# The even sums of block 12 made on GpSimd: one line of an order written out by hand

## The chip, the cores and the metric

The kernel runs on one core of a Trainium2 chip. A core has five engines that run their own instruction streams and wait for one another through semaphores: TensorE (PE in the profile, its weight loads PEld), VectorE (DVE), ScalarE (ACT), GpSimd (POOL) and SyncE (SP, which here issues nearly all of the transfers). The metric is the device time of one execution in microseconds (us). The time before the change is 439.48 us, the median of three runs (439.42 to 439.49).

## The reference

The reference is a spectral mixing layer followed by a gated feed-forward layer, in float32, on one sequence of 2048 rows of 512 numbers:

```python
def _A_ref(x, w_r, w_i):
    X = rfft2(x); W = w_r + 1j * w_i
    return irfft2(X * W, (S, D))
def _B_ref(x, w_gate, w_up, w_down):
    h = gelu(x @ w_gate) * (x @ w_up)
    return h @ w_down
h  = x + _A_ref(layernorm(x), A_w_r, A_w_i)
h2 = h + _B_ref(layernorm(h), B_w_gate, B_w_up, B_w_down)
```

So the first half normalizes every row, takes a two-dimensional Fourier transform over rows and columns, multiplies by a filter, transforms back and adds the input. The second half normalizes again, multiplies by two matrices (512 x 1376), gates, and multiplies back.

## The kernel before

The 2048 rows lie as 16 blocks of 128 rows, one row of each block per partition. The Fourier transforms are products with small tables of cosines and sines on TensorE. The kernel goes through these stages: a transform over the rows, block by block (called the first stage here); a transform over the columns, the filter and the inner transform back (the second stage, lines 427 to 474); the transform back over the rows (lines 535 and 874); and the feed-forward layer, which takes most of the time (lines 165 to 167, 774 and 1113).

In the first stage a block b goes through these steps, each of which has a letter in a list called START; a letter followed by a number is one step on one block:

- `f`: the fold. A row's 512 numbers are cut into two halves, and their difference and their sum are written to the tile `pn` (lines 340 and 341). Blocks 12 and 13 are folded together by one pair of instructions, and so are 2 and 3, 4 and 5, and so on up to 10 and 11; blocks 0, 1, 14 and 15 are folded alone. GpSimd does it for all but block 15, which VectorE folds (ON_VECTOR).
- `v`: the second fold. VectorE takes the difference of the two quarters of `pn` and writes it to `uv` (line 351), for both blocks of a pair at once. The odd column frequencies need it.
- `u`: the second sum. The two quarters of `pn` of one block are added and written to `us` (line 361). The even column frequencies can be made from it. It is an optional step: only blocks 13, 14 and 15 have it before the change, on VectorE.
- `s`, `g`, `m`, `q`, `r`, `n`: the mean and the variance of the rows and the root of the variance; `c`: the table of cosines and sines of the block is multiplied by that root and written to `ms` (line 332, on ScalarE).
- `a`: the even frequencies on TensorE (line 374), and `b`: the odd ones. `b` is two products of 128 by 128. `a` is two products where the block has had its step `u`, and four where it has not, because then the two quarters are added up by TensorE in PSUM, each quarter with a product of its own. TensorE takes a float32 product as two records in the profile, so two products are a row `x4` there and four are `x8`.
- `k`: ScalarE copies the block's bank of PSUM to the tile `ts` (line 382); for block 15 half of it is copied by VectorE (`l`, line 385), after a small memset of a PSUM region (`z`, line 389).

What makes the sum `u` is in these lines:

```python
us = w1.tile([P, 2, P], F32, name="us", bufs=5)
eng = pool if b in SUMS_ON_POOL else dve
eng.tensor_tensor(us, pn[:, :, 0], pn[:, :, 1], op=ALU.add)
parts[b][:2] = [[us[:, 0]], [us[:, 1]]]
```

The order of the steps on TensorE, ScalarE, VectorE and GpSimd is the order of START, word for word: each engine takes its own steps in the order in which they stand there, and waits at a step until what the step reads is there. On GpSimd there are also two small additions for the filter's edge columns (`wh`, line 483), which belong to the second stage and stand in the program right behind the fold of block 14; behind them come the subtractions that prepare the weights of the feed-forward layer (`raw`, lines 209 to 217), and the first of these waits for the last second fold on VectorE (line 351).

The second stage begins with line 427 on TensorE, which reads `ts` of all blocks. Its first products need the copies of the even half of block 15, which VectorE makes (line 385), and ScalarE's copies of all earlier blocks.

Of the kernel before, what the change touches and what calls it, by code (L numbers as in the profile page):

```python
# [35 lines left out]
START = """  # L36
f0 s0 g0 r0 n0 s1 c0 v0 g1 s2 m3 q3 r1 g2 f1 v1 n1 r2 m5 c1 q5 n2 c2 m7 c3 f2 s4 s6 g4 a0 b0 w7 g6 v2 q7 r4 n4 m9 c4
s8 c5 c6 q9 a1 a2 b1 a3 f4 f6 m11 b2 k0 v4 s10 q11 g10 g8 c7 v6 b3 a4 f8 a5 b5 b4 r8 k2 k1 n8 c8 s12 f10 a6 m13 c9 c10
c11 k4 a7 b7 f12 f14 q13 s15 v8 g12 s14 k3 b6 k7 g15 a8 a9 k5 g14 r12 v10 n12 b8 v12 b9 k9 c12 a11 u13 c13 a10 b10 u14
k8 f15 b11 a12 b12 k6 a13 k10 c14 c15 k11 v14 u15 b13 k13 k12 v15 a14 b14 a15 b15 z4 l15 k14 k15  # L40
"""

ON_POOL = ()

ON_VECTOR = (15,)

SUMS_ON_POOL = ()

ROOTS = {0: 1, 1: 1, 2: 2, 4: 4, 8: 4, 12: 4}

# [71 lines left out]
def kernel(  # L122
# [114 lines left out]
    with (  # L237
# [119 lines left out]
        def sums2(b):  # L357
            pn = pns[group[b][0]][:, b - group[b][0]]
# [3 lines that stand above are left out]
# [1074 lines left out]
```

## Time and profile before

| what | value |
|---|---|
| median of three runs | 439.48 us |
| the profiled execution | 439.26 us |
| its span, first to last instruction | 437.0 us |
| TensorE busy | 431.5 us, 99% of the span |
| GpSimd busy, VectorE busy, ScalarE busy | 314.4, 312.6 and 242.8 us |
| first product of the first stage (line 374) | at 7.50 us |
| first product of the second stage (line 427) | at 29.97 us |

Times in the profile count from the first instruction of the span. A row of the timeline gives the start, the duration, the engine, the line, the operation, what it writes and reads, the shape, and, in brackets at the end, how long the engine had been idle before it and what ended that. Instructions of one kind that follow each other are merged into one row (`x4`). Instructions overlap a little at their ends, so the step from one start to the next tells the pace of an engine better than a duration does, above all for TensorE. The chain of work that ended last is followed back from the last instruction, at each step to whatever released it.

### The profile page before, as it was taken

The page shows a single profiled execution, that of the slowest core. Times are in us where ns is not written, and L with a number is a line of the kernel's source. Part 1 is how long each engine was busy: PE and PEld are TensorE (multiplying, and loading weights), DVE is VectorE, ACT ScalarE, POOL GpSimd, SP SyncE. Part 2 cuts the span into 40 slices and gives each one's busy share as a digit, 9 for nine tenths or more (in the row PEclk, how much of TensorE's full clock was granted, in tenths as well). Part 3 has the DMA queues.
Part 4 walks back from the last instruction along what each step waited for, and adds up shares of the span by engine and source line. Part 5 has one row for each costly group of instructions (what it writes and reads, how often), then busy time and mean ns, then how long its engine had stood idle before and what let it go on. Part 6 is the DMA issues. An engine that isn't in the chain of part 4 may idle for free.

```text
span 437.0 us, 6628 instructions
## 1 busy us (share of the span) xinstructions
PE 431.5 (99%) x2275; PEld 367.4 (84%) x2275; DVE 312.6 (72%) x578; ACT 242.8 (56%) x503; POOL 314.4 (72%) x346
## 2 busy tenths in 40 slices
PE   8999999999999999999999999999999999999996
PEld 8999999789978777877888888888888888888885
DVE  5979976898764766378735579478677787687786
ACT  5989685799802441124432786376455653575640
POOL 6988896999957788558653844067879779787821
PEclk9999999999999999999999999999999999999999
DMA  8996914220032122112230203401212021200005
GB/s 285 392 413 77 398 35 152 109 73 24 1 121 97 49 71 75 48 49 72 72 73 24 73 25 127 162 16 57 73 48 73 29 69 49 72 25 2 0 2 193
DMA packets 23542, 41.60 MB, mean 95 GB/s; under 512 B 4178, under 2 KB 9810, under 8 KB 23380
## 3 DMA queue, kind: packets, MB, share of 16 engines
q1 hardware_dynamic: 23220, 40.92, 27.8%
q8 instruction: 18, 0.29, 0.3%
q10 hardware_dynamic: 288, 0.26, 0.2%
q14 instruction: 16, 0.13, 0.1%
HBM read 36.97 MB, written 4.20 MB: 94 GB/s over the span
## 4 chain that ended last, share of the span: by engine, by line
PE 98%; issue 0%; DVE 0%; ACT 0%; POOL 0%; DVEq 0%; POOLq 0%
PE ps L165 16%; PE ps L166 16%; PE ps L167 16%; PE ps L774 14%; PE ps L1113 11%; PE ps L374 5%; PE ps L427 3%; PE ps L535 3%; PE ps L442 3%; PE ps L469 3%; PE ps L176 2%; PE ps L874 2%; PE ps L982 1%; PE ps L1219 1%; PE ps L568 1%; PE ps L574 1%
## 5 line engine op out<-in xcount | busy, mean ns | idle before, releaser
L165 PE MATMUL ps<-cb,gu 128*128 128x512 f32 (+1 forms) x336 | 127.4, 379 | 0.0
L167 PE MATMUL ps<-cb,gu 128*128 128x512 f32 (+1 forms) x336 | 124.9, 372 | 0.0
L166 PE MATMUL ps<-cb,gu 128*128 128x512 f32 (+1 forms) x336 | 124.8, 371 | 0.0
L678 ACT ACTIVATE s<-ps 128x512 f32<-128x512 f32 (+1 forms) x72 | 40.2, 560 | 87.2 <-PE ps L167 86.9
L230 POOL TENSOR_TENSOR gu<-raw,gu 128x768 fp32r<-128x768 f32 (+1 forms) x42 | 61.3, 1479 | 30.3 <-DVE gu L225 17.7
L165 PEld LDWEIGHTS ps<-cb,gu 128*128 128x128 f32 x336 | 63.3, 188 | 11.8 <-issue 1.0
L166 PEld LDWEIGHTS ps<-cb,gu 128*128 128x128 f32 x336 | 63.3, 188 | 11.7 <-issue 1.0
L167 PEld LDWEIGHTS ps<-cb,gu 128*128 128x128 f32 x336 | 63.2, 188 | 11.0
L774 PE MATMUL ps<-wd,a 128*128 128x512 f32 x264 | 63.6, 393 | 0.0
L774 PEld LDWEIGHTS ps<-wd,a 128*128 128x128 f32 x264 | 49.2, 188 | 11.5 <-DVE gh L983 0.9
L687 DVE TENSOR_TENSOR ps<-ps,s 128x512 f32<-128x512 f32 (+1 forms) x48 | 31.2, 651 | 27.8 <-PE ps L167 25.7
L1120 DVE TENSOR_TENSOR gh<-ps,gh 128x512 f32<-128x512 f32 x66 | 44.2, 680 | 0.8 <-PE ps L1113 0.8
L684 ACT ACTIVATE s<-s 128x512 f32<-128x512 f32 (+1 forms) x48 | 28.5, 594 | 20.6 <-DVE s L681 20.5
L780 DVE TENSOR_TENSOR gh<-ps,gh 128x512 f32<-128x512 f32 x24 | 16.5, 689 | 27.0 <-PE ps L774 26.9
L681 DVE TENSOR_TENSOR s<-ps,s 128x512 f32<-128x512 f32 (+1 forms) x48 | 30.8, 641 | 5.9 <-PE ps L167 4.7
L516 POOL TENSOR_TENSOR wd<-wdr,wd 128x512 fp32r<-128x512 f32 x12 | 15.5, 1294 | 18.9 <-ACT wd L514 18.9
L681 DVE TENSOR_TENSOR ps<-ps,s 128x512 f32<-128x512 f32 (+1 forms) x24 | 15.7, 652 | 16.8 <-ACT s L678 16.6
L1026 POOL TENSOR_TENSOR t<-mis,t 128x768 fp32r<-128x768 f32 (+1 forms) x9 | 13.3, 1480 | 13.3 <-ACT t L1024 13.2
L693 ACT ACTIVATE a<-ps 128x512 fp32r<-128x512 f32 (+1 forms) x26 | 13.7, 532 | 15.6 <-DVE ps L687 15.6
L458 POOL TENSOR_TENSOR z<-t,t 128x520 f32<-128x520 f32 x15 | 19.5, 1297 | 2.7 <-DVE t L450 2.1
L209 POOL TENSOR_TENSOR raw<-raw 128x256 f32<-128x256 f32 x16 | 11.8, 739 | 12.4 <-DMA raw<-in_wgu 10.7
L434 ACT ACTIVATE dp<-ps 64x512 f32<-64x512 f32 x30 | 17.7, 591 | 4.8 <-PE ps L427 4.5
(184 smaller groups left out, 899.3 us busy)
## 6 DMA issues: line engine op xcount, KB each, us to landing
wt<-in_w SPq DMA_DIRECT2D x16, 520.0 KB, 7.4
raw<-in_wgu SPq DMA_DIRECT2D x32, 256.0 KB, 3.0
out<-gh SPq DMA_DIRECT2D x15, 256.0 KB, 2.0
gh<-in_x SPq DMA_DIRECT2D x7, 512.0 KB, 9.1
row<-in_x SPq DMA_DIRECT2D x12, 256.0 KB, 2.7
wdr<-in_wd SPq DMA_DIRECT2D x12, 256.0 KB, 2.7
mis<-in_wd SPq DMA_DIRECT2D x10, 256.0 KB, 2.5
a<-in_wgu SPq DMA_DIRECT2D x8, 256.0 KB, 3.1
```

The costliest lines, as they stand in the source:

```text
L165: pe.matmul(o, lh, rh, start=(i == 0 and not onto), stop=False, skip_group_check=True)
L166: pe.matmul(o, lh, rl, start=False, stop=False, skip_group_check=True)
L167: last = pe.matmul(o, ll, rh, start=False, stop=(i == n - 1), skip_group_check=True)
L230: pooled["lo"] = pool.tensor_tensor(r[:, 1, m], t[:, m], r[:, 0, m].bitcast(F32), op=ALU.subtract)
L374: pe.matmul(spectrum(b, c)[:, c], o, mc, start=(z == 0), stop=(z == len(parts[b][c]) - 1))
L678: return lambda: act.activation(to, a, AF.Copy)
L681: return lambda: dve.tensor_tensor(to, a, b, op=ALU.add)
L684: return lambda: act.activation(g, g, AF.Gelu_apprx_tanh)
L687: return lambda: dve.tensor_tensor(u, u, g, op=ALU.mult)
L774: pe.matmul(o, parts_of[tiles.index((0, f))][:, ha, i // 4, r], wds[f][:, hw, c], start=start, stop=stop)
L1113: pe.matmul(ps[:, k], w[:, hw], a[ha], start=start and hw + ha == 0, stop=hw == 1, skip_group_check=True)
L1120: by.tensor_tensor(to, o, to, op=ALU.add)
```

## The change

Block 12 gets a step `u`, on GpSimd, and its step `a` moves to a later place among TensorE's steps. In the list START the step `u12` is put in behind `a11`, and `a12` is moved from between `b11` and `b12` to behind `b13`.

```diff
-c11 k4 a7 b7 f12 f14 q13 s15 v8 g12 s14 k3 b6 k7 g15 a8 a9 k5 g14 r12 v10 n12 b8 v12 b9 k9 c12 a11 u13 c13 a10 b10 u14
-k8 f15 b11 a12 b12 k6 a13 k10 c14 c15 k11 v14 u15 b13 k13 k12 v15 a14 b14 a15 b15 z4 l15 k14 k15
+c11 k4 a7 b7 f12 f14 q13 s15 v8 g12 s14 k3 b6 k7 g15 a8 a9 k5 g14 r12 v10 n12 b8 v12 b9 k9 c12 a11 u12 u13 c13 a10 b10
+u14 k8 f15 b11 b12 k6 a13 k10 c14 c15 k11 v14 u15 b13 a12 k13 k12 v15 a14 b14 a15 b15 z4 l15 k14 k15
...
-SUMS_ON_POOL = ()
+SUMS_ON_POOL = (12,)
```

On TensorE, at the end of the first stage, the rows are the products of blocks 11, 10, 12, 13, 14 and 15, in the order of the program; a row names the table (`ms`), the folded data (`pn`, `uv` or `us`) and the number of products. `pn_340` and `uv_379` belong to blocks 12 and 13, `ms_384` is the table of block 12. Before:

```order
L374 MATMUL ps_72<-ms_329,uv_372 128x128 x2
L374 MATMUL ps_72<-ms_331,uv_372 128x128 x2
L374 MATMUL ps_72<-ms_384,pn_340 128x128 x4
L374 MATMUL ps_72<-ms_384,uv_379 128x128 x2
L374 MATMUL ps_72<-ms_392,us_390 128x128 x2
L374 MATMUL ps_72<-ms_392,uv_379 128x128 x2
L374 MATMUL ps_72<-ms_418,us_400 128x128 x2
L374 MATMUL ps_72<-ms_418,uv_423 128x128 x2
L374 MATMUL ps_72<-ms_420,us_425 128x128 x2
```

These rows are b10, b11, a12, b12, a13, b13, a14, b14 and a15. The same place in the changed kernel, where the sums of blocks 12, 13, 14 and 15 are `us_390`, `us_392`, `us_402` and `us_423`:

```order
L374 MATMUL ps_72<-ms_329,uv_372 128x128 x2
L374 MATMUL ps_72<-ms_331,uv_372 128x128 x2
L374 MATMUL ps_72<-ms_384,uv_379 128x128 x2
L374 MATMUL ps_72<-ms_394,us_392 128x128 x2
L374 MATMUL ps_72<-ms_394,uv_379 128x128 x2
L374 MATMUL ps_72<-ms_384,us_390 128x128 x2
L374 MATMUL ps_72<-ms_416,us_402 128x128 x2
L374 MATMUL ps_72<-ms_416,uv_421 128x128 x2
L374 MATMUL ps_72<-ms_418,us_423 128x128 x2
```

The four products of a12 are gone from their place ahead of b12, and two products that read `us_390` stand between b13 and a14.

On GpSimd, at the end of its folds, this is the difference between the two programs, with one row more in the changed one:

```order
 L341 TENSOR_TENSOR pn_343<-gh_58 128x256
 L483 TENSOR_TENSOR wh_447<-ws_133 128x16x4 x2
+L361 TENSOR_TENSOR us_390<-pn_340 128x256
 L209 TENSOR_TENSOR raw_135<-raw_135 128x256
 L213 TENSOR_TENSOR raw_135<-raw_135 128x256
```

The new sum stands behind the fold of block 14 and behind the two additions for `wh`, and ahead of the preparation of the weights. VectorE, ScalarE and SyncE have the same rows in the same order in both programs.

## The prediction

> **What bounds the kernel now.** I read the page's busy times first, then the chain of work that ended last, then the timeline of TensorE, VectorE and GpSimd where the first stage ends. The page:
>
> ```profile
> span 437.0 us, 6628 instructions
> PE 431.5 (99%) x2275; PEld 367.4 (84%) x2275; DVE 312.6 (72%) x578; ACT 242.8 (56%) x503; POOL 314.4 (72%) x346
> PE 98%; issue 0%; DVE 0%; ACT 0%; POOL 0%; DVEq 0%; POOLq 0%
> ```
>
> TensorE is busy 99% of the span and holds 98% of the chain. So a delay of TensorE early on is carried to the end, unless a later stretch of the chain waits for something that isn't delayed. These are the longest pieces of the chain that are not TensorE's work after 25 us:
>
> ```profile
> 72.54 0.88 ACT gh L474 x2
> 123.67 0.76 DVE gh L983
> 432.58 0.57 issue
> 433.15 0.41 DVE gh L1224
> 433.57 0.33 DVEq L1428
> ```
>
> None of them is a transfer; each works on what TensorE has just made. Next, TensorE's rows where the change is made:
>
> ```profile
> 25.14 1.06 PE L374 MATMUL ps<-ms,pn 128*128 128x128 f32 x8
> 26.04 0.61 PE L374 MATMUL ps<-ms,uv 128*128 128x128 f32 x4
> 26.75 0.68 PE L374 MATMUL ps<-ms,us 128*128 128x128 f32 x4
> 27.27 0.61 PE L374 MATMUL ps<-ms,uv 128*128 128x128 f32 x4
> 27.71 0.61 PE L374 MATMUL ps<-ms,us 128*128 128x128 f32 x4
> 28.25 0.71 PE L374 MATMUL ps<-ms,uv 128*128 128x128 f32 x4
> 28.80 0.61 PE L374 MATMUL ps<-ms,us 128*128 128x128 f32 x4
> 29.24 0.61 PE L374 MATMUL ps<-ms,uv 128*128 128x128 f32 x4
> 29.97 0.35 PE L427 MATMUL ps<-dfs,ts 128*128 128x128 f32 x1
> ```
>
> In order these are a12, b12, a13, b13, a14, b14, a15, b15 and the second stage's first product. The starts give the pace: 8 records (a12) take 0.90 us, 4 records 0.44 (27.27 to 27.71). There are three waits: b12's four slots were over at 26.48 and a13 began at 26.75; a14 was done at 28.15 and b14 began at 28.25; L427 began 0.29 after b15's last slot (29.68). What was waited for stands on the other engines (the GpSimd row at 28.94 is the first preparation of the weights):
>
> ```profile
> 24.45 0.73 POOL L340 TENSOR_TENSOR pn<-gh 128x256 f32<-128x256 f32 x1
> 24.52 1.20 DVE L351 TENSOR_TENSOR uv<-pn 128x512 f32<-128x512 f32 x1 [0.68 <-POOL pn L341]
> 25.14 1.18 POOL L341 TENSOR_TENSOR pn<-gh 128x256 f32<-128x256 f32 x1
> 25.65 0.95 DVE L361 TENSOR_TENSOR us<-pn 128x256 f32<-128x256 f32 x1
> 26.28 0.50 POOL L483 TENSOR_TENSOR wh<-ws 128x64 f32<-128x64 f32 x1
> 26.52 0.53 DVE L361 TENSOR_TENSOR us<-pn 128x256 f32<-128x256 f32 x1
> 26.74 0.50 POOL L483 TENSOR_TENSOR wh<-ws 128x64 f32<-128x64 f32 x1
> 26.98 0.54 DVE L340 TENSOR_TENSOR pn<-gh 128x256 f32<-128x256 f32 x1
> 27.44 0.41 DVE L341 TENSOR_TENSOR pn<-gh 128x256 f32<-128x256 f32 x1
> 27.78 0.41 DVE L351 TENSOR_TENSOR uv<-pn 128x256 f32<-128x256 f32 x1
> 28.11 0.41 DVE L361 TENSOR_TENSOR us<-pn 128x256 f32<-128x256 f32 x1
> 28.45 0.41 DVE L351 TENSOR_TENSOR uv<-pn 128x256 f32<-128x256 f32 x1
> 28.94 0.72 POOL L209 TENSOR_TENSOR raw<-raw 128x256 f32<-128x256 f32 x1 [1.70 <-DVE uv L351]
> 29.07 0.07 DVE L389 MEMSET ps<- 128x16 f32 x1 [0.21 <-ACT ts L382]
> 29.44 0.42 DVE L385 COPY ts<-ps 128x256 f32<-128x256 f32 x1 [0.30 <-PE ps L374]
> ```
>
> VectorE's rows are v12 (24.52, for blocks 12 and 13), u13, u14, the two folds of block 15, v14, u15, v15, the memset and the copy l15. GpSimd's are the fold of block 14, the two `wh`, and the weights. a13 waited for u13, which ended at 26.60; b14 for v14 (28.19); L427 for l15 (29.86).
>
> The same rows show how the two engines get in each other's way. Alone, a sum of 128x256 takes VectorE 0.41 us (27.44) and GpSimd 0.73 (24.45). Side by side they take turns: the second half of f14 on GpSimd spans 1.18 us and ends 0.60 after v12 (26.32 against 25.72); u13 then spans 0.95 and ends 0.28 after it (26.60); `wh`, u14, `wh` and the first fold of block 15 go on in the same way, the last two ending at 27.24 and 27.52. So an instruction of one engine holds the other's up until it is nearly over.
>
> **The change part by part.**
>
> *Products taken out.* a12 falls from 8 records to 4: 0.90 - 0.45 = 0.45 us less work. Where it stood, nothing is gained by that. b12 now follows b11 at 25.14 and needs v12, which still ends at 25.72; with 0.06 to 0.15 of handing over (v14 ended at 28.19 and b14 began at 28.25; u13 ended at 26.60 and a13 began at 26.75) it begins near 25.85 and is done near 26.38. a13 still waits for u13 and begins at 26.75 as before, since nothing ahead of u13 on VectorE or GpSimd changes. So the old four products of a12 ran in time in which TensorE has to wait for VectorE in any case, and the new two come behind that wait.
>
> *The floor of the loss.* Suppose u12 were ready when TensorE gets there, at 27.71 behind b13. Then a12, a14 and b14 take 3 x 0.45 and a15 begins at 29.05 instead of 28.80. The wait and the slow restart at b14 (28.15 to 28.25, and 0.55 instead of 0.45 for its records, 0.20 in all) are covered by the 0.45 of a12, so 0.25 is left as a loss.
>
> *When u12 is ready.* On GpSimd it stands behind the second `wh`. That ends at 27.24, and by then the first fold of block 15 has been waiting on VectorE since 26.98. By the taking of turns in the rows above VectorE goes next, until 27.52, and u12 ends 0.60 later as f14 did behind v12: 28.12. The trace has no sum of two quarters on GpSimd. Its lower bound is the 0.73 of a fold of the same size alone (27.24 + 0.73 = 27.97, if it gets in ahead of VectorE), the upper one 27.52 + 0.73 = 28.25, if it can't begin before VectorE's fold is over. I take 28.12, since the nearest row, a GpSimd sum of the same size right behind a VectorE sum, has just this case.
>
> *The wait that is added.* a12 begins at 28.12 + 0.06 = 28.18, so TensorE waits 0.47 behind b13. Behind a12 on TensorE stand a14, b14, a15, b15 and the whole second stage. With a restart like that of b14 (0.55 from 28.25 to 28.80) a14 begins at 28.73, b14 at 29.17, a15 at 29.62. Before, a15 began at 28.80: 0.82 later. l15 and L427 follow a15 at the same distance, so L427 begins at 30.79.
>
> *What u12 does to VectorE.* The second fold of block 15 asks at 27.44, is held until u12 is over and ends 0.28 after it, at 28.40 instead of 27.85. v14, u15 and v15 move by the same 0.55 and end at 28.74, 29.08 and 29.41. They are wanted at 29.17 (b14), 29.62 (a15) and 30.06 (b15), so they cost nothing, with 0.4 to 0.6 us to spare. The weights on GpSimd wait for v15 and begin 0.55 later too, while TensorE and all that it releases move by 0.82, so this is covered by a quarter of a microsecond more than before.
>
> *Copies and the memset.* ScalarE's copies of k13, k12 and k14:
>
> ```profile
> 27.91 1.68 ACT L382 ACTIVATE ts<-ps 128x512 f32<-128x512 f32 x3 [0.82 <-PE ps L374]
> ```
>
> Their order stays. k12 now waits for a12, whose records are done at 28.18 + 0.71 = 28.89, and ends after its 0.56 (a third of the row) near 29.5; the memset follows it at 29.6, ahead of l15, which can't begin before a15's records are done at 29.62 + 0.61 = 30.23. No cost. No transfer is moved, and SyncE's list is the same.
>
> *The sum.* The loss of a12's place 0.25, and the wait for u12 with its restart 0.57, together 0.82. The profiled execution took 439.26 us, 437.0 of it the span and 2.3 around it, which the change doesn't touch; with 0.82 it would be 440.08. It lies 0.22 under the median of the runs, so against that median of 439.48 I forecast 440.30 us, 0.19% more.
>
> **A rule beside the rows.** The Trainium skill, in SBUF — State Buffer, section "Who interferes with whom", says that a VectorE instruction with two inputs in SBUF and a GpSimd instruction that reads SBUF exclude each other, and that the later one blocks fully until the first has finished. The taking of turns agrees with it; the end of f14 only 0.60 after v12, where alone it takes 0.73, does not quite. By the strict rule u12 would end at 28.25 and the sum would be 0.95.
>
> **The rivals.**
>
> 1. *The strict turn: slower by more than 0.2%.* If u12 starts only when the fold of block 15 is over, its full 0.73 stands behind 27.52. Everything behind a12 is 0.13 later: 0.95 in all, 440.43. It decides as soon as u12 ends later than 28.18, where the loss passes 0.88 us, 0.2% of 439.48; about that much is what a measurement of this kernel can tell from no change. For it speaks that the fold alone takes 0.73; against it, f14's 0.60. This is the rule of the skill above. Chance 0.13.
> 2. *GpSimd goes first.* u12 holds on directly behind `wh` and the fold of block 15 waits. u12 ends at 27.97, a12 begins at 28.03, the loss is 0.67, 440.15. Six instructions in a row that alternate speak against it. Chance 0.10.
> 3. *Later stages take it back.* The pieces at 72.54 and 123.67 give 1.64 us in which TensorE is not the chain. Should what they wait for not move with TensorE, they could swallow the 0.82 or part of it: about 439.75. Against it: both are copies or sums of TensorE's own results. Even all of it would need 0.82 + 0.88 = 1.70 to end faster by 0.2%, more than there is. Chance 0.10, and 0.04 beside it for a faster kernel by something that I don't see.
> 4. *The delay grows.* Another turn of VectorE and GpSimd in the second stage, shifted by 0.27 against each other, costs one more held sum: 0.95 - 0.41 = 0.54 us as for u13, 440.84 at most. Chance 0.08.
>
> **How the numbers follow.** My forecast has 0.55, with its own range of 440.15 to 440.45; of it I count 0.15 above 440.36, where slower by 0.2% begins, since the distance is only 0.06. Slower: 0.15 + 0.13 + 0.08 = 0.36. Faster: 0.04. Within 0.2%: 0.60. The range 440.00 to 440.60 leaves out the third rival with the faster case (0.14) and half of the fourth (0.04).
>
> **What the profile of the changed kernel would show.** TensorE's a13 at 26.75 as before, with a longer idle time ahead of b12 near 25.2 to 25.8; a GpSimd row L361 that ends near 28.1; the second fold of block 15 on VectorE near 0.95 long instead of 0.41; a12 as `x4` at 28.2; a15 near 29.6 and L427 near 30.8. An L427 at 30.8 with an unchanged end would mean that the third rival holds; a GpSimd row that ends by 27.7 would leave only the floor of 0.25; an L427 below 30.0 would make the whole reading wrong.

## The result and the profile after

The changed kernel takes 440.13 us in the median of 22 runs (439.86 to 440.44), the kernel before 439.38 (439.18 to 439.62, 22 runs on the same chips). The ratio is 1.0017, with a 95% interval of 1.0011 to 1.0023: slower by 0.75 us. The profiled execution took 440.06 us, its span is 437.8.

The page after, its span and its chain of work by engine:

```profile
span 437.8 us, 6619 instructions
PE 92%; POOL 5%; DMA 1%; issue 1%; DVE 0%; ACT 0%; DVEq 0%
```

GpSimd had 0% of the chain before. The chain in order of time, from 25 us on, shows what is on it:

```profile
25.19 1.18 POOL pn L341
26.36 0.92 POOL wh L483 x2
27.28 0.87 POOL us L361
28.16 0.04 issue
28.20 2.50 PE ps L374 x20
30.70 0.12 issue
30.82 1.24 PE ps L427 x9
```

TensorE's last 20 records of the first stage (a12, a14, b14, a15 and b15) wait for the new sum, that one stands behind `wh`, and `wh` behind the folds. The share of the chain alone doesn't show that the new sum is the cause: GpSimd holds 4% of it also in an experiment below that adds no sum to GpSimd (order only), since a13 waits, by way of u13, for the same folds. What the new sum costs is read from the rows. These are TensorE's rows there:

```profile
25.93 0.68 PE L374 MATMUL ps<-ms,uv 128*128 128x128 f32 x4 [0.66 <-DVE uv L351]
26.80 0.68 PE L374 MATMUL ps<-ms,us 128*128 128x128 f32 x4 [0.19 <-DVE us L361]
27.31 0.61 PE L374 MATMUL ps<-ms,uv 128*128 128x128 f32 x4
28.20 1.16 PE L374 MATMUL ps<-ms,us 128*128 128x128 f32 x8 [0.28 <-POOL us L361]
29.20 0.61 PE L374 MATMUL ps<-ms,uv 128*128 128x128 f32 x4
29.64 0.61 PE L374 MATMUL ps<-ms,us 128*128 128x128 f32 x4
30.09 0.61 PE L374 MATMUL ps<-ms,uv 128*128 128x128 f32 x4
30.82 0.35 PE L427 MATMUL ps<-dfs,ts 128*128 128x128 f32 x1
```

The rows are b12, a13, b13, a12 with a14 (`x8`), b14, a15, b15 and the second stage. And these are GpSimd's and VectorE's rows beside them:

```profile
24.50 0.72 POOL L340 TENSOR_TENSOR pn<-gh 128x256 f32<-128x256 f32 x1
25.19 1.18 POOL L341 TENSOR_TENSOR pn<-gh 128x256 f32<-128x256 f32 x1
26.32 0.96 POOL L483 TENSOR_TENSOR wh<-ws 128x64 f32<-128x64 f32 x2
27.25 0.90 POOL L361 TENSOR_TENSOR us<-pn 128x256 f32<-128x256 f32 x1
...
27.03 0.54 DVE L340 TENSOR_TENSOR pn<-gh 128x256 f32<-128x256 f32 x1
27.49 0.94 DVE L341 TENSOR_TENSOR pn<-gh 128x256 f32<-128x256 f32 x1
28.35 0.41 DVE L351 TENSOR_TENSOR uv<-pn 128x256 f32<-128x256 f32 x1
28.69 0.41 DVE L361 TENSOR_TENSOR us<-pn 128x256 f32<-128x256 f32 x1
29.02 0.41 DVE L351 TENSOR_TENSOR uv<-pn 128x256 f32<-128x256 f32 x1
29.62 0.07 DVE L389 MEMSET ps<- 128x16 f32 x1 [0.19 <-ACT ts L382]
30.29 0.42 DVE L385 COPY ts<-ps 128x256 f32<-128x256 f32 x1 [0.60 <-PE ps L374]
```

The fold of block 15 is two instructions, L340 and L341, which are called its first and second fold here (step `v`, L351, is another thing). The sum u12 spans 0.90 us and ends at 28.15, 0.58 behind VectorE's first fold of block 15 (27.57). The second fold is held up until then, spans 0.94 and ends at 28.43.

Everything here starts 0.05 later than in the profile before (24.50 against 24.45 for the fold of block 14); that much arises ahead of the place of the change, and it differs from profile to profile (the fold starts between 24.45 and 24.60 in the ten of them). So below I measure from the start of that fold (the GpSimd row L340 of 128x256) to the first product of the second stage (L427), and call it the stretch. Before it is 29.97 - 24.45 = 5.52 us, after 30.82 - 24.50 = 6.32: 0.80 us more. The span grew by 0.8 too (437.0 to 437.8): from L427 to its end are 407.0 us in both, so the later stages carry the delay to the end.

One profile is taken of each kernel, so it matters how well such a distance repeats. Where the order of v12 and u13 is left as it was, in eight of the ten profiles, a13 begins 2.28 to 2.30 us behind the fold. Behind L427 the scatter is larger: to the end of the last sum (L1224) it takes 403.9 to 404.0 us.

### The profile page after: what moved, and what is told of

Read it like the earlier page. It is cut to its first block, busy times and chain, and to the rows that moved or that the text cites. A ratio compares the mean times of both kernels' runs of the same rounds, so it can differ in the third digit from the quotient of the medians.

```text
span 437.8 us, 6619 instructions
## 1 busy us (share of the span) xinstructions
PE 431.2 (98%) x2271; PEld 366.7 (84%) x2271; DVE 312.9 (71%) x578; ACT 242.7 (55%) x503; POOL 315.3 (72%) x347
## 4 chain that ended last, share of the span: by engine, by line
PE 92%; POOL 5%; DMA 1%; issue 1%; DVE 0%; ACT 0%; DVEq 0%
PE ps L165 16%; PE ps L167 16%; PE ps L166 16%; PE ps L774 14%; PE ps L1113 11%; PE ps L427 3%; PE ps L535 3%; PE ps L442 3%; PE ps L469 3%; POOL pn L341 2%; POOL pn L340 2%; PE ps L874 2%; PE ps L982 1%; PE ps L1219 1%; PE ps L568 1%; PE ps L574 1%
```

## The experiments

Each kernel is timed in rounds beside the kernel before on the same chip, and the ratio is to that; the first row is the comparison above. Medians are of 11 executions (22 for the change, 5 for the sum twice). The stretch is from the profile, one execution of each kernel, and what was expected stands for the stretch:

| kernel | median, us | before, us | ratio (95% interval) | stretch, us | against before | expected |
|---|---|---|---|---|---|---|
| the change | 440.13 | 439.38 | 1.0017 (1.0011 to 1.0023) | 6.32 | +0.80 | +0.82 |
| order only | 440.13 | 439.42 | 1.0017 (1.0008 to 1.0026) | 6.21 | +0.69 | +0.70 |
| sum only | 439.90 | 439.42 | 1.0011 (1.0003 to 1.0020) | 6.04 | +0.52 | +0.55 |
| sum ahead of `wh` | 439.66 | 439.42 | 1.0005 (0.9996 to 1.0014) | 5.79 | +0.27 | +0.25 |
| `wh` late | 439.20 | 439.42 | 0.9995 (0.9986 to 1.0004) | 5.32 | -0.20 | -0.19 |
| no a12 | 439.46 | 439.43 | 1.0002 (0.9993 to 1.0010) | 5.51 | -0.01 | 0 |
| sum twice | 441.04 | 439.43 | 1.0037 (1.0023 to 1.0051) | 7.18 | +1.66 | +1.68 |
| u13 first, k6 misplaced | 439.62 | 439.43 | 1.0004 (0.9995 to 1.0013) | 5.83 | +0.31 | -0.26 |
| u13 first | 439.04 | 439.48 | 0.9989 (0.9980 to 0.9998) | 5.27 | -0.25 | -0.26 |

### Were the old products free? a12 left out

```diff
-k8 f15 b11 a12 b12 k6 a13 ...
+k8 f15 b11 b12 k6 a13 ...
```

> The kernel before with the four products of a12 left out, so the even frequencies of block 12 are not made; everything else is as before. My theory: those products ran in time in which TensorE waits for v12 and u13 in any case; b12 begins near 25.9, a13 at the same time as before, 0.15 behind the end of u13, and the second stage is not a bit earlier: ratio 1.0000. The rival theory, that TensorE is the bound there and its work counts: 0.89 us less, ratio 0.9980.

TensorE's rows of this kernel, b12, a13, b13 and, after the mark, the second stage:

```profile
25.92 0.68 PE L374 MATMUL ps<-ms,uv 128*128 128x128 f32 x4 [0.65 <-DVE uv L351]
26.79 0.68 PE L374 MATMUL ps<-ms,us 128*128 128x128 f32 x4 [0.19 <-ACT ms L332]
27.31 0.61 PE L374 MATMUL ps<-ms,uv 128*128 128x128 f32 x4
...
30.01 1.69 PE L427 MATMUL ps<-dfs,ts 128*128 128x128 f32 x13
```

Where a12 was there is an idle time of 0.65 us ahead of b12, and a13 begins 2.29 us behind the fold (26.79 - 24.50) as before (26.75 - 24.45 = 2.30). The row of a13 names ScalarE (`ms`, L332) as what ended the wait; those are the tables of blocks 14 and 15, which a13 doesn't read. They end at 26.64, and u13 at 26.65: the profile names one of two that ended together, and the last experiment shows that the wait is for VectorE. The second stage gains nothing. So the 0.89 us of products that the change halves were worth nothing in their place.

### The order alone

```diff
-k8 f15 b11 a12 b12 k6 a13 k10 c14 c15 k11 v14 u15 b13 k13 ...
+k8 f15 b11 b12 k6 a13 k10 c14 c15 k11 v14 u15 b13 a12 k13 ...
```

> The change without the sum u12: block 12's even frequencies are made by four products from pn, as before, but at the later place, behind b13. My theory: the old four products ran while TensorE has to wait for u13 anyway, so behind that wait their 0.89 us count in full, less the 0.20 of the wait at b14 that they cover: a15 and the second stage begin 0.70 us later than before, ratio 1.0016. The rival theory, that the loss comes from GpSimd's sum and from what it does to VectorE: no change, ratio 1.0000, since VectorE and GpSimd run as before.

a12 with its four products, behind b13, then a14 and, after the mark, the second stage:

```profile
27.82 1.06 PE L374 MATMUL ps<-ms,pn 128*128 128x128 f32 x8
28.71 0.61 PE L374 MATMUL ps<-ms,us 128*128 128x128 f32 x4
...
30.78 0.46 PE L427 MATMUL ps<-dfs,ts 128*128 128x128 f32 x2
```

The 0.89 us from 27.82 to 28.71 now count, less the wait at b14 that they cover: +0.69 (30.78 - 24.57 = 6.21 against 5.52). VectorE and GpSimd have the same rows as before, and GpSimd makes no new sum; the rival theory, which expected no change, falls. Moving a12 with its old four products behind the wait for u13 costs nearly as much as the whole change, which has two products there and the wait for the sum.

### The sum alone

```diff
-... a11 u13 c13 a10 b10 u14
+... a11 x12 u13 c13 a10 b10 u14
...
+"x": lambda b: pool.tensor_tensor(w1.tile([P, 2, P], F32, name="us", bufs=5), pns[b][:, 0, :, 0], pns[b][:, 0, :, 1], op=ALU.add),
```

> The kernel before, with the sum of block 12's quarters made on GpSimd at the place of the change, but read by nobody; TensorE keeps its old order and products. My theory: the sum holds up the second fold of block 15 on VectorE, v14 ends near 28.75 instead of 28.19, and b14, which in the old order wants it at 28.15, waits: the second stage begins 0.55 us later, ratio 1.0012. The rival theory, that only TensorE's order and its wait for u12 cost anything and GpSimd's work is off the path: ratio 1.0000.

VectorE's second fold of block 15 and v14, and TensorE's b14 and second stage in this kernel:

```profile
27.59 0.94 DVE L341 TENSOR_TENSOR pn<-gh 128x256 f32<-128x256 f32 x1
28.45 0.41 DVE L351 TENSOR_TENSOR uv<-pn 128x256 f32<-128x256 f32 x1
...
28.92 0.71 PE L374 MATMUL ps<-ms,uv 128*128 128x128 f32 x4 [0.45 <-DVE uv L351]
...
30.64 0.57 PE L427 MATMUL ps<-dfs,ts 128*128 128x128 f32 x3
```

The second fold is held up (0.94 instead of 0.41), v14 ends at 28.86, and b14 waits for it: +0.52 (30.64 - 24.60 = 6.04). So a sum on GpSimd that nobody reads delays TensorE through VectorE. In the change itself the same hold-up of VectorE costs nothing: v14 is done at 28.76 there, and TensorE, which has waited for u12, comes to b14 only at 29.20.

### The sum ahead of `wh`

```diff
-pool.tensor_tensor(wh[:, :, m], ws[:, 0, :, m], ws[:, 1, :, m], op=op)
+behind(pool.tensor_tensor(wh[:, :, m], ws[:, 0, :, m], ws[:, 1, :, m], op=op), lasts)
```

This is made in the changed kernel; `lasts` is v15.

> The change, but with the two additions for wh put behind v15, so that u12 stands directly behind the fold of block 14. My theory: u12 ends near 27.2, before TensorE is through with b13 at 27.71, VectorE's later sums run alone, and only the floor is left: 0.25 us later than before, ratio 1.0006. A rival theory, that the whole loss is u12's lateness: ratio 1.0000. Another, that GpSimd's sum costs the same wherever it stands: ratio 1.0017, as the change.

GpSimd's u12, TensorE's a12 with a14, and the second stage in this kernel:

```profile
26.33 0.91 POOL L361 TENSOR_TENSOR us<-pn 128x256 f32<-128x256 f32 x1
...
27.76 1.06 PE L374 MATMUL ps<-ms,us 128*128 128x128 f32 x8
...
30.30 0.91 PE L427 MATMUL ps<-dfs,ts 128*128 128x128 f32 x6
```

u12 ends at 27.24, TensorE goes on behind b13 without a wait, and 0.27 of the loss is left (30.30 - 24.51 = 5.79). It separates the two terms of the sum: the floor, from the place of a12, and the rest of 0.53, from a sum that stands behind two small additions and waits its turn. The ratio itself, 1.0005, doesn't exclude 1; the profile's stretch is what decides. The kernel differs from the one before in the place of `wh` as well, which by itself is worth 0.20 (next experiment). Against that kernel it takes 0.47 more (5.79 - 5.32), which is the whole time of a12's two products.

### `wh` late in the kernel before

The same line in the kernel before, and nothing else.

> The kernel before, with nothing changed but the two additions for wh, which wait for v15. My theory: u14 and the first fold of block 15 run alone, v14 ends near 27.95 instead of 28.19, the wait at b14 and its restart are gone: the second stage begins 0.19 us earlier, ratio 0.9996. The rival theory, that VectorE and GpSimd don't hold each other up but are slowed by something else there (transfers, say): ratio 1.0000 and VectorE's rows as long as before.

VectorE's u13 with u14, the two folds of block 15 and v14, GpSimd's `wh`, and the second stage in this kernel:

```profile
25.74 1.28 DVE L361 TENSOR_TENSOR us<-pn 128x256 f32<-128x256 f32 x2
26.95 0.41 DVE L340 TENSOR_TENSOR pn<-gh 128x256 f32<-128x256 f32 x1
27.29 0.41 DVE L341 TENSOR_TENSOR pn<-gh 128x256 f32<-128x256 f32 x1
27.62 0.41 DVE L351 TENSOR_TENSOR uv<-pn 128x256 f32<-128x256 f32 x1
...
28.78 0.60 POOL L483 TENSOR_TENSOR wh<-ws 128x64 f32<-128x64 f32 x2 [2.37 <-DVE uv L351]
...
29.87 1.35 PE L427 MATMUL ps<-dfs,ts 128*128 128x128 f32 x10
```

The first fold takes 0.41 us instead of 0.54, v14 begins 3.07 us behind the fold of block 14 (27.62 - 24.55) instead of 3.33 (27.78 - 24.45), and b14 no longer waits: -0.20 (29.87 - 24.55 = 5.32). The ratio, 0.9995, doesn't exclude 1 here either. That VectorE's long rows come from GpSimd's work beside them is shown by this: the same instructions are short as soon as `wh` stands elsewhere.

### The sum twice

```diff
-... a11 u12 u13 c13 a10 b10
+... a11 x12 u12 u13 c13 a10 b10
```

This is made in the changed kernel, with the step `x` as above.

> The change with one more sum of the same size on GpSimd ahead of u12, whose result nobody reads. My theory, by turns: the first sum ends where u12 ended (28.12 in the frame of the profile before), the second fold of block 15 comes next and ends 0.28 later, and u12 ends 0.60 behind that, near 29.0; the second stage begins 1.68 us later than in the kernel before, ratio 1.0038. If GpSimd took two sums in a row, u12 would end near 28.85 and the ratio would be 1.0035; by a strict exclusion with the full 0.73 each time, 1.96 us and 1.0045.

GpSimd's two sums, VectorE's two folds of block 15 and v14, and the second stage:

```profile
27.26 0.90 POOL L402 TENSOR_TENSOR us<-pn 128x256 f32<-128x256 f32 x1
28.13 0.90 POOL L361 TENSOR_TENSOR us<-pn 128x256 f32<-128x256 f32 x1
...
27.05 0.54 DVE L340 TENSOR_TENSOR pn<-gh 128x256 f32<-128x256 f32 x1
27.51 0.94 DVE L341 TENSOR_TENSOR pn<-gh 128x256 f32<-128x256 f32 x1
28.37 0.94 DVE L351 TENSOR_TENSOR uv<-pn 128x256 f32<-128x256 f32 x1
...
31.70 0.35 PE L427 MATMUL ps<-dfs,ts 128*128 128x128 f32 x1
```

The first sum ends at 28.16, the second fold at 28.45, the second sum at 29.03, v14 at 29.31: turn for turn, with 0.28 to 0.29 for VectorE's and 0.58 for GpSimd's instruction behind the other's end. The delay is 1.66 us (31.70 - 24.52 = 7.18), where two GpSimd sums in a row would give 1.54 and the full 0.73 for each GpSimd sum 1.96.

### u13 first

Two kernels put u13 ahead of v12 and a13 ahead of b12, with `wh` late as above. The first of them also had ScalarE's copy k6 behind a13. That was an oversight of mine: a13 writes the bank that k6 copies, so in this kernel the even columns of block 6 are those of block 13.

```diff
-... b8 v12 b9 k9 c12 a11 u13 c13 a10 b10 u14
-k8 f15 b11 a12 b12 k6 a13 k10 ...
+... b8 u13 v12 b9 k9 c12 a11 c13 a10 b10 u14
+k8 f15 b11 a12 a13 b12 k6 k10 ...
```

> The kernel before with the additions for wh behind v15, and beside it u13 ahead of v12 on VectorE, and a13 ahead of b12 on TensorE. My theory: a13 then runs behind a12 without a wait, b12 waits for v12, which ends near 26.60, and a15 begins 0.26 us earlier than in the kernel before, 0.06 more than with wh alone moved: ratio 0.9994. The rival theory, that the wait at a13 isn't for VectorE: the exchange changes nothing, ratio 0.9996 as with wh alone.

It came out 0.31 us later instead of 0.26 earlier, because ScalarE now waited 1.54 us for a13, with its copies k6 and k10 and the tables of blocks 14 and 15 behind that wait:

```profile
26.64 1.09 ACT L382 ACTIVATE ts<-ps 128x512 f32<-128x512 f32 x2 [1.54 <-PE ps L374]
27.61 0.69 ACT L332 ACTIVATE ms<-mfs,rs 128x128 f32<-128x128 f32 x2
```

The tables of blocks 14 and 15 are made at 27.61, and a14, which needs the first of them, began at 28.07; the second stage in turn waited for ScalarE's copies. So its time tests nothing of the theory. The second kernel has k6 back in its place:

```diff
-k8 f15 b11 a12 a13 b12 k6 k10 ...
+k8 f15 b11 a12 k6 a13 b12 k10 ...
```

> As the experiment with u13 first, with ScalarE's copy k6 back ahead of a13, which overwrites its bank: the kernel before with wh behind v15, u13 ahead of v12 on VectorE and a13 ahead of b12 on TensorE, ScalarE's order as before. My theory: a13 follows a12 without a wait, b12 waits for v12 (which ends near 26.60), b13, a14, b14 and a15 follow without a wait, and a15 begins 0.26 us earlier than in the kernel before: ratio 0.9994. The rival theory, that the wait at a13 isn't for VectorE: no more than wh alone gives, ratio 0.9996.

TensorE's a12, a13, b12 with b13, and the second stage:

```profile
25.15 1.06 PE L374 MATMUL ps<-ms,pn 128*128 128x128 f32 x8
26.05 0.61 PE L374 MATMUL ps<-ms,us 128*128 128x128 f32 x4
26.77 1.16 PE L374 MATMUL ps<-ms,uv 128*128 128x128 f32 x8
...
29.84 1.91 PE L427 MATMUL ps<-dfs,ts 128*128 128x128 f32 x15
```

a13 follows a12 without a wait, and the wait for VectorE is now at b12 (26.50 to 26.77). So the wait at a13 was for VectorE. The stretch is 0.25 shorter than before (29.84 - 24.57 = 5.27), 0.05 shorter than with `wh` late alone. This version is a little faster than the kernel before: 439.04 us, ratio 0.9989 with an interval of 0.9980 to 0.9998. The median gained more (0.44) than the stretch; the interval holds the stretch's 0.25 (0.9994), and whether there is more than that isn't settled.

## Why the prediction was right

The forecast was 440.30 us, 0.82 more than before. Measured were 440.13, which is 0.75 more in the median, and 0.80 more in the profile. Of the 0.17 between the two times, 0.10 is the kernel before, whose median is 439.38 over 22 runs and was 439.48 over the three that the forecast started from.

- *Products taken out.* Right that nothing is gained by it in its place, and shown by leaving them out altogether: -0.01. b12 began 1.43 behind the fold of block 14 (25.93 - 24.50), as worked out (25.85 - 24.45 = 1.40), and a13 didn't move (2.30 in both).
- *The floor of 0.25.* Right: 0.27 with the sum early.
- *When u12 is ready.* Right: 28.10 in the frame of the profile before (28.15 less 0.05), predicted 28.12. The nearest row, the second half of f14 behind v12, gave 0.60 for what took 0.58.
- *The added wait and its restart.* Right: a12 began 3.70 behind the fold (28.20 - 24.50), worked out were 3.73, and a15 1.44 behind a12 in both. That is a15 0.79 later than before (5.14 against 4.35 behind the fold) where 0.82 was forecast.
- *VectorE's delay is covered.* Right: v15 ended at 29.43 and was wanted at 30.09. The sum alone, where the same delay costs 0.52, shows that it was covered only because TensorE came to b14 later.
- *Copies, memset, weights.* Right: the memset ran at 29.62, and l15 at 30.29 still had to wait for a15 (idle 0.60, ended by TensorE). The weights began 0.53 later (29.52 - 24.50 = 5.02 behind the fold against 28.94 - 24.45 = 4.49), where 0.55 was forecast.

Of the rivals, the strict turn falls with u12's end at 28.10 instead of 28.25 and with the sum twice (1.66, not 1.96). Its price was itself too low: 28.25 takes the fold's end as the rows show it, 27.52. Held to full durations on both engines, the fold would end at 27.24 + 0.41 = 27.65 and u12 at 28.38, for a loss of 1.08. That is further still from what was measured. GpSimd going first falls with the same rows. That later stages take the delay back, or add to it, falls with the 407.0 us behind L427 in both profiles and with the median's 0.75. The statement that a measurement tells about 0.2% from no change was too careful: the interval of the change is 0.06% to either side, so that a loss of 0.17% was told apart from none.

The Trainium skill's rule, in SBUF — State Buffer, section "Who interferes with whom", of full blocking until the first instruction has finished, agrees with the order of the turns in every run here, and gives a turn that is too long: u12 ended 0.58 behind VectorE's fold, where alone a GpSimd sum of this size takes 0.72 to 0.73.

## What to carry to other kernels

Before work is taken from an engine that is busy all the time, ask whether the engine would not wait in its place anyway, and what the same work costs at its new place: here half of it behind a wait was dearer than all of it ahead of one. Where VectorE and GpSimd both add tiles in SBUF and both have something waiting, count their instructions as one queue with alternating turns, and look for small ones that stand in the way of those that TensorE waits for; here two additions of 64 columns put off by 2.4 us (28.78 - 24.55 = 4.23 behind the fold instead of 26.28 - 24.45 = 1.83) gave 0.20 us in the stretch.

## What I had not expected

That VectorE and GpSimd alternate so strictly: in the sum twice, twelve instructions took turns with no exception (from the fold of block 14 to v14). Where one had waited for the other, it ended at nearly the same distance behind the other's end in all ten profiles: 0.28 to 0.29 us for a VectorE sum of 256 columns, and 0.58 to 0.59 for GpSimd's. That is less than the durations alone (0.41, and 0.72 to 0.73). It is also less than the step from one such sum to the next on the same engine: 0.34 on VectorE (27.44, 27.78, 28.11 in the rows before) and 0.69 on GpSimd (24.45, 25.14). Why a turn is shorter than a step stays open. Not every instruction of VectorE takes part in the turns: its copy l15, which reads PSUM, ran beside GpSimd's subtractions for the weights and took 0.42 in the profile before as in the one after, and those took 0.72 to 0.73, no more than a GpSimd sum of this size alone.

And that the chain of work tells so little about the cause of a small delay. GpSimd's share of it went from 0% to 5% with the change, but it is 4% in order only, where GpSimd has no new sum, and the chain of no a12 runs through ScalarE and VectorE instead. At a13 several waits end within a few hundredths of a microsecond of each other, and the chain follows whichever the profile puts last.
